# Scores and S^T over 128 contracted rows instead of 96 and 98, in a kernel of attention beside a Fourier transform

## The chip, the core and the metric

The kernel runs on one core of a Trainium2 chip. A core has five engines that run side by side, each with its own queue of instructions: TensorE (PE, matrix products; its loads of the stationary operand are shown apart as PEld), VectorE (DVE), ScalarE (ACT), GpSimd (POOL) and SyncE (SP), whose queue issues this kernel's DMAs. On-chip memory is SBUF, with 128 partitions; products go to PSUM, which has 8 banks of 128 x 512 single-precision numbers. A product multiplies a stationary tile (contracted rows x 128 columns) with a moving tile (contracted rows x up to 512 columns); the contracted rows lie on the partitions.

The metric is the device time of one execution in microseconds, the median of several runs.

## What is computed

Two layers stand side by side in the output: full attention with 32 heads on A, and the real part of a two-dimensional Fourier transform, as products with given matrices, on B. Cut to what matters:

```python
def _A_ref(x, wqkv, wo):                      # x: 1 x 2048 x 1024
    H = 32; Dh = D // H                       # 32 heads of 32
    qkv = (x @ wqkv).reshape(B, S, 3, H, Dh).transpose(2, 0, 3, 1, 4)
    q, k, v = qkv[0], qkv[1], qkv[2]
    p = _softmax(jnp.einsum("bhqd,bhkd->bhqk", q, k) * Dh ** -0.5, axis=-1)
    o = jnp.einsum("bhqk,bhkd->bhqd", p, v)
    return o.transpose(0, 2, 1, 3).reshape(B, S, D) @ wo

def _B_ref(x, dft_seq_re, dft_seq_im, dft_hid_re, dft_hid_im):
    a = jnp.einsum("bsd,ed->bse", x, dft_hid_re)
    b = jnp.einsum("bsd,ed->bse", x, dft_hid_im)
    return jnp.einsum("ts,bse->bte", dft_seq_re, a) - jnp.einsum("ts,bse->bte", dft_seq_im, b)
```

## The kernel before

**The dense products** (q, k, v, the two Fourier stages, the output projection) are Strassen-like products of blocks. Each operand is split into a high and a low part of a shorter float format, and each product of blocks is made of three matmuls (high x high, low x high, high x low) that add up in one PSUM bank: groups of 12 or 24 matmuls, all over 128 rows, issued at line 380. They go by the name of fills, because they are put between the matmuls of the attention.

**The attention** runs head by head. A head's q and k lie in SBUF as three blocks of 32 rows each, so that one product over 96 rows sums the high and low combinations (`qk_d` is laid out for this). There are two sets of tiles, `QS[0]`, `KS[0]` and `QS[1]`, `KS[1]`, of 98 partitions x 2048, and head h uses set h % 2. For each head:

- `scores` (PE line 1185) makes 32 blocks of 128 queries x 1024 keys, two matmuls each, contracted over rows 0 to 95. VectorE takes the negated maximum of each block (line 1191), ScalarE the exponential and its sum (line 1194), in place in the PSUM tile `psS`, of which there are two. For heads after the first, the first four blocks of queries come from a tile of their own, `qx` (96 x 512, loaded at line 1170), because `QS` is still in use by the head two before.
- When the 32 maxima are there, their high and low parts are turned, written to `m_d` and read back into rows 96 and 97 of `QS` (lines 1232 and 1233). Rows 96 and 97 of `KS` hold ones.
- `transposed` (PE line 1308) makes S^T, 64 matmuls of 128 keys x 512 queries, contracted over rows 0 to 97: the last two rows subtract the maximum. ScalarE takes the exponential (line 1312) out of two `psT` banks into SBUF.
- P V (PE line 1327) follows after every four tiles of keys: 32 matmuls in a row, 128 rows x 32 columns stationary, placed in four column groups of the array. Four such sections belong to a head.

While S^T of head h runs, the scores of head h + 1 run too. When the last S^T matmul of head h is done, the loads of q for head h + 2 are issued (four DMAs of 192 KB, line 291), and those of v behind them (line 1285); k was loaded in quarters before.

**The order** of all instructions is written out by a list scheduler in the program, the class `Plan` and the loop from line 1387 on. It knows each operation's cost (a matmul 0.229 us, a score block's maximum 1.22, its exponential 1.235, a DMA's issue 0.46) and what it depends on; at each step it gives TensorE a matmul of the attention if one is ready, and a fill otherwise. The other engines' queues are filled in the same run, in the order of rank and readiness; SP's operations carry the size of the transfer. Each engine's order is then fixed, and the engines wait for each other through semaphores. Memsets and DMAs that are written ahead of the scheduler (lines 279 to 283) or when a pool of tiles is first asked for (`att`, lines 304 to 315) stand in their engine's queue at that place without being in the plan.

Ahead of everything stand the first set of tiles, two memsets on POOL (the ones in `KS[0]` and `rec`, whose right half is only there to fill a transposition), and then the first loads on SP. `att` makes the second set of tiles as soon as the memory of the first stage is free.

Of the kernel before, what the change touches and what calls it, by code (L numbers as in the profile page):

```python
# [8 lines left out]
F32 = mybir.dt.float32  # L9
# [52 lines left out]
class Plan:  # L62
# [23 lines left out]
    def op(self, engine, cost, emit, after=(), uses=(), rank=0.0, kb=0, order=None, other=None, lanes=1, two=False):  # L86

        o = Op(engine, cost, emit, rank, kb, other, two)  # L90
        o.lanes = lanes
        seen = set()
        for d in after:
            if d is not None and id(d) not in seen:
                seen.add(id(d))
                self._wait(o, d)
        for u in uses:
            u.append(o)
        if order is not None:
            p, order.first = order.first, o  # L100
            if p is not None and not p.begun:
                p.soon.append(o)
                o.left += 1
        if o.left == 0:
            self._release(o)
        return o
# [104 lines left out]
def kernel(  # L211
# [19 lines left out]

    r_d = [dram.tile([2 * NS, P], F32, name=f"r_d{h}") for h in range(H)]
    m_d = [dram.tile([2 * NS, P], F32, name=f"m_d{h}") for h in range(H)]

    o_d = [dram.tile([P, 4, NB], F32, name=f"o_d{c}") for c in range(NC)]
    ab_d = [[[dram.tile([P, NB], F32, name=f"ab_d{m}_{e}_{k}") for k in range(NS)] for e in range(2)] for m in range(2)]
# [12 lines left out]
    def f(ap):  # L249
        return ap.bitcast(F32)  # L250
# [25 lines left out]
            nc.sync.dma_start(d[:, 0:2, :] if b % 2 else d[:, 0:3:2, :], f(t).rearrange("p (o n) -> p o n", o=1).broadcast_to([P, 2, NB]))  # L276


    qk0 = tc.alloc_tile_pool(name="qk0", bufs=1, side="right")
    QS, KS = [qk0.tile([98, S], F32R, name="qs0")], [qk0.tile([98, S], F32R, name="ks0")]  # L280
    nc.gpsimd.memset(f(KS[0])[96:98, :], 1.0)
    rec = const.tile([P, 2 * NS], F32, name="rec")
    nc.gpsimd.memset(rec, 1.0)

    def load_qk(h, which, j):
# [18 lines left out]
    def att():  # L304

        if "att" not in late:
            vp.release()
            vph.release()
            late["sums"] = ctx.enter_context(tc.tile_pool(name="sums", bufs=1, reuse_waits="tile"))
            late["atl"] = tc.alloc_tile_pool(name="atl", bufs=1, reuse_waits="tile")  # L310
            late["att"] = a = tc.alloc_tile_pool(name="att", bufs=1, side="right", reuse_waits="tile")
            QS.append(a.tile([98, S], F32R, name="qs1"))
            KS.append(a.tile([98, S], F32R, name="ks1"))
            nc.gpsimd.memset(f(KS[1])[96:98, :], 1.0)
        return late["att"]

# [839 lines left out]
    def load_qk_op(h, which, j, after):  # L1156
        g = h // 4
        got[h, which, j] = op("SP", ISSUE, lambda: load_qk(h, which, j), [*qk_st[2 * g + which][j], *after], [], -2, 192)

    def scores(h):  # L1160
        ST = {}
        sold, suse = small["st"].take()
        maxes, exps = [], []
        if h:
            xold, xuse = qx_r.take()

            def load_x():
                qx["t"] = att().tile([96, NB], F32R, name="qx")
                g, r0 = divmod(h, 4)
                nc.sync.dma_start(f(qx["t"]), qk_d[2 * g][0][r0 * DH : r0 * DH + DH].rearrange("d i c -> (d i) c"))  # L1170

            got[h, "x"] = op("SP", ISSUE, load_x, [*xold, *qk_st[2 * (h // 4)][0], *(att_gate if h == 1 else [])], [xuse], -2, 192)
        qx = {}
        for n, (qt, c) in enumerate([(k % 4, k // 4) for k in range(8)] + [divmod(k, 2) for k in range(8, 32)]):
            old, users = psS_r.take()
            own = h > 0 and qt < 4
            box = {}

            def mm(n=n, qt=qt, c=c, box=box, own=own):
                if n == 0:  # L1180
                    ST["negm"] = sm.tile([P, 2, NS], F32, name="negm", bufs=2)
                    ST["sums"] = sm.tile([P, 2, NS], F32, name="sums", bufs=2)
                box["p"] = p = psS.tile([P, 1024], F32, name="psS")
                for i in range(2):
                    nc.tensor.matmul(  # L1185
                        p[:, i * NB : i * NB + NB], (qx["t"] if own else QS[h % 2][0:96])[:, qt * P : qt * P + P],
                        KS[h % 2][0:96, c * 1024 + i * NB : c * 1024 + i * NB + NB], start=True, stop=True,
                    )

            def mx(qt=qt, c=c, box=box):  # L1190
                nc.vector.tensor_reduce(out=ST["negm"][:, c, qt : qt + 1], in_=box["p"], axis=AX.X, op=ALU.max, negate=True)  # L1191

            def ex(qt=qt, c=c, box=box):
                nc.scalar.activation(box["p"], box["p"], AF.Exp, bias=ST["negm"][:, c, qt : qt + 1], accum_out=ST["sums"][:, c, qt : qt + 1])  # L1194

            a = op("PE", 2 * MM, mm, [*old, got.get((h, "x") if own else (h, 0, qt // 4)), got.get((h, 1, 2 * c)), got.get((h, 1, 2 * c + 1))],
                   [users, xuse] if own else [users])
            b = op("DVE", MAX, mx, [a] + (sold if n == 0 else []), [users, suse], 0)
            e = op("ACT", ES, ex, [b], [users, suse], 0)
            exp_of[a] = e  # L1200
            maxes.append(b)
            exps.append(e)
            Sops.setdefault(h, []).append(a)
            streams["S"].append((a, h, n))
            if n == 5 and h:
                sums(h - 1)

        nold, nuse = small["nm"].take()
        lold, luse = small["lh"].take()
        box = {}  # L1210

        def nmin():
            ST["nm"] = sm.tile([P, NS], F32, name="nm", bufs=2)
            nc.vector.tensor_reduce(out=ST["nm"], in_=ST["negm"].rearrange("p c n -> p n c"), axis=AX.X, op=ALU.min)

        def high():
            box["l"] = sm.tile([P, 2, NS], F32R, name="lh", bufs=2)
            nc.vector.tensor_reduce(out=box["l"][:, 0], in_=ST["negm"].rearrange("p c n -> p n c"), axis=AX.X, op=ALU.min)

        def low():  # L1220
            nc.vector.tensor_tensor(out=box["l"][:, 1], in0=ST["nm"], in1=f(box["l"])[:, 0], op=ALU.subtract)

        b = op("DVE", TINY, high, maxes + lold, [luse, suse], -2)
        a = op("DVE", TINY, nmin, maxes + nold, [nuse, suse], -2)
        c = op("DVE", TINY, low, [a, b], [nuse, luse], -2, two=True)
        def across():
            box["t"] = sm.tile([P, 2 * NS], F32, name="lt", bufs=2)
            nc.vector.transpose(box["t"], f(box["l"]).rearrange("p i s -> p (i s)"))

        d = op("DVE", TINY, across, [b, c], [luse], -2)  # L1230

        put = op("SP", ISSUE, lambda: nc.sync.dma_start(m_d[h].rearrange("i (g p) -> g i p", g=4), box["t"]), [d], [luse], -3, 32)
        moved = [op("SP", ISSUE, lambda: nc.sync.dma_start(f(QS[h % 2])[96:98, :], m_d[h].rearrange("(i q) p -> i (q p)", i=2)), [put], [], -3, 16)]
        mine[h] = (ST, suse, nuse, exps, moved)
# [59 lines left out]
    def transposed(h):  # L1294
# [4 lines left out]
        for t in range(NS):  # L1299
            for j in range(4):  # L1300
                old, users = psT_r.take()
                here = pt_r.n % NPT < NLOW
                pold, puse = pt_r.take()
                box = {}

                def mm(t=t, j=j, box=box):
                    box["p"] = psT.tile([P, NB], F32, name="psT")
                    nc.tensor.matmul(box["p"], KS[h % 2][0:98, t * P : t * P + P], QS[h % 2][0:98, j * NB : j * NB + NB], start=True, stop=True)  # L1308

                def ex(box=box, here=here):  # L1310
                    box["t"] = att_low().tile([P, NB], F32, name="ptl", bufs=NLOW) if here else att().tile([P, NB], F32, name="pt", bufs=NPT - NLOW)
                    nc.scalar.activation(box["t"], box["p"], AF.Exp)  # L1312

                a = op("PE", MM, mm, [*old, *moved, *(att_gate if h == t == j == 0 else []), *(got.get((h, w, k)) for w, k in ((0, j), (1, t // 4)))], [users])
                e = op("ACT", ET, ex, [a, *pold], [users, puse], 0, 0, pt_r)
                exp_of[a] = e
                streams["T"].append((a, h, 4 * t + j))
                Tops.setdefault(h, []).append(a)
                todo.append((t, j, box, e, puse))
# [26 lines left out]
        if h + 2 < H:  # L1346
            for j in range(4):
                load_qk_op(h + 2, 0, j, [Tops[h][-1], Sops[h][-1]])
            load_v(h + 2)
        return e, po, ouse  # L1350

# [145 lines left out]
```

## Time and profile before

| | |
|---|---|
| median of 3 runs | 3041.0 us (3037.66 to 3042.22) |
| the profiled execution | 3036.63 us; its span, first to last instruction, 3034.8 us |
| TensorE busy | 3010.0 us, 14912 matmuls |
| VectorE busy | 2435.1 us |
| ScalarE busy | 2293.7 us |
| POOL busy | 840.5 us |
| mean granted TensorE clock | 0.998 of full speed |
| matmuls of the fills, L380 | 6720, over 128 rows |
| scores, L1185 | 2048, over 96 rows |
| S^T, L1308 | 2048, over 98 rows |
| P V, L1327 | 4096, over 128 rows, 32 columns |

How to read the rows of the profile: a group or a timeline row names the engine, the line of the kernel, the operation, the tile written <- the tiles read, then rows*columns of a matmul's stationary operand and the shape of the moving one, and a count. In the timeline the first number is the start in us from the start of the span, the second the time from the start of the first to the end of the last instruction of that row, and like instructions that follow each other share one row. In a group the numbers behind the bar are the busy time in us, the mean length of one in ns, and the engine's idle time ahead of it with what ended that. Matmuls overlap: one is listed with some 0.39 us from its start to its modelled end, while the next starts well before that. A row of the windows view gives the stretch, its length, each engine's busy time and count, the granted clock, the share of the DMA engines and GB/s. A row of waits gives who waited for whom, the sum in us, how often, and the longest.

### The profile page before, as it was taken

The page shows a single profiled execution, that of the slowest core. Times are in us where ns is not written, and L with a number is a line of the kernel's source. Part 1 is how long each engine was busy: PE and PEld are TensorE (multiplying, and loading weights), DVE is VectorE, ACT ScalarE, POOL GpSimd, SP SyncE. Part 2 cuts the span into 40 slices and gives each one's busy share as a digit, 9 for nine tenths or more (in the row PEclk, how much of TensorE's full clock was granted, in tenths as well). Part 3 has the DMA queues.
Part 4 walks back from the last instruction along what each step waited for, and adds up shares of the span by engine and source line. Part 5 has one row for each costly group of instructions (what it writes and reads, how often), then busy time and mean ns, then how long its engine had stood idle before and what let it go on. Part 6 is the DMA issues. An engine that isn't in the chain of part 4 may idle for free.

```text
span 3034.8 us, 45369 instructions
## 1 busy us (share of the span) xinstructions
PE 3010.0 (99%) x14912; PEld 2149.4 (71%) x14912; DVE 2435.1 (80%) x3283; ACT 2293.7 (76%) x4316; POOL 840.5 (28%) x619
## 2 busy tenths in 40 slices
PE   9999999999999999999999999999999999999999
PEld 7887666667666766677666766676666766676787
DVE  7778789778878877887678888888777889887696
ACT  4347888888888888888888888888888887776331
POOL 2302234322202321231021344332111244332152
PEclk9999999999999999999999999999999999999999
DMA  9974558766615644554434675545433587556662
GB/s 346 352 219 147 181 167 265 243 214 223 222 58 175 204 130 146 187 180 140 139 108 142 207 245 167 163 147 169 126 110 90 158 272 223 157 176 198 228 230 102
DMA packets 376313, 558.06 MB, mean 184 GB/s; under 512 B 110896, under 2 KB 110896, under 8 KB 376016
## 3 DMA queue, kind: packets, MB, share of 16 engines
q1 hardware_dynamic: 376080, 555.17, 57.3%
q8 instruction: 120, 1.97, 0.3%
q14 instruction: 113, 0.93, 0.1%
HBM read 401.93 MB, written 153.09 MB: 183 GB/s over the span
## 4 chain that ended last, share of the span: by engine, by line
PE 92%; DVE 5%; ACT 1%; DMA 1%; issue 1%; POOL 0%; SPq 0%; ACTq 0%; DVEq 0%; POOLq 0%
PE pd L380 41%; PE psT L1308 15%; PE psS L1185 15%; PE pd L1327 14%; PE psT L380 7%; DVE negm L1191 2%; ACT psS L1194 1%; DVE slot L466 1%; DVE raw L444 1%; DVE slot L469 0%; DMA g<-in_ct 0%; DVE h L466 0%; DVE l L469 0%; DMA raw<-in_xb 0%; DVE e L896 0%
## 5 line engine op out<-in xcount | busy, mean ns | idle before, releaser
L1191 DVE TENSOR_REDUCE negm<-psS 128x1 f32<-128x1024 f32 x1024 | 1238.6, 1219 | 207.1 <-PE psS L1185 201.4
L1194 ACT ACTIVATE psS<-psS,negm 128x1024 f32<-128x1024 f32 x1024 | 1140.4, 1114 | 104.5 <-DVE negm L1191 98.5
L1312 ACT ACTIVATE pt<-psT 128x512 f32<-128x512 f32 x1668 | 940.0, 621 | 318.0 <-PE psT L1308 316.7
L380 PE MATMUL pd<-slot,h 128*128 128x512 f32 x3368 | 1168.0, 395 | 1.4 <-DVE h L466 1.4
L1308 PE MATMUL psT<-qs,ks 98*128 98x512 f32 x2048 | 815.3, 403 | 1.3 <-ACT pt L1312 1.3
L380 PEld LDWEIGHTS pd<-slot,h 128*128 128x128 f32 x3368 | 637.4, 189 | 156.8 <-issue 7.5
L380 PE MATMUL pd<-slot,l 128*128 128x512 f32 x1684 | 664.3, 394 | 0.0
L1308 PEld LDWEIGHTS psT<-qs,ks 98*128 98x128 f32 x2048 | 383.9, 189 | 187.5 <-issue 80.5
L1185 PE MATMUL psS<-ks,qs 96*128 96x512 f32 x1552 | 479.7, 398 | 5.9 <-ACT psS L1194 5.5
L1327 PE MATMUL pd<-pt,vt 128*32 128x512 f32 x3336 | 437.2, 596 | 1.3 <-DVE e L670 0.7
L469 POOL TENSOR_TENSOR l<-raw,h 128x512 fp32r<-128x512 f32 x137 | 186.4, 1361 | 825.0 <-PE psT L1308 297.6
L444 POOL TENSOR_TENSOR raw<-raw,g 128x512 f32<-128x512 f32 x215 | 285.0, 1331 | 440.5 <-DMA raw<-in_ct 74.1
L380 PEld LDWEIGHTS pd<-slot,l 128*128 128x128 f32 x1684 | 319.0, 189 | 76.1 <-issue 3.4
L1185 PEld LDWEIGHTS psS<-ks,qs 96*128 96x128 f32 x1552 | 291.7, 189 | 77.7 <-ACT psS L1194 15.5
L469 POOL TENSOR_TENSOR slot<-raw,slot 128x512 fp32r<-128x512 f32 x148 | 212.7, 1444 | 431.7 <-DVE slot L466 291.3
L1327 PEld LDWEIGHTS pd<-pt,vt 128*32 128x32 f32 x3336 | 108.5, 110 | 227.0 <-issue 212.9
L1312 ACT ACTIVATE ptl<-psT 128x512 f32<-128x512 f32 x380 | 219.1, 627 | 59.4 <-PE psT L1308 59.1
L1194 ACT ACTIVATION_READ_ACCUMULATOR psS<-psS,negm 128x1 f32 x1024 | 235.3, 230 | 0.0
L1340 DVE TENSOR_TENSOR ot<-ot,pd 128x512 f32<-128x512 f32 x96 | 65.9, 686 | 169.3 <-PE pd L1327 169.3
L380 PE MATMUL pd<-slot,slot 128*128 128x512 f32 x768 | 194.3, 391 | 0.2 <-DVE ot L1340 0.2
L380 PEld LDWEIGHTS pd<-slot,slot 128*128 128x128 f32 x768 | 144.3, 188 | 31.3 <-DVE ot L1340 0.6
L466 DVE CAST h<-raw 128x512 fp32r<-128x512 f32 x321 | 148.3, 463 | 19.9 <-PE pd L380 16.6
(116 smaller groups left out, 2262.5 us busy)
## 6 DMA issues: line engine op xcount, KB each, us to landing
raw<-in_ct SPq DMA_DIRECT2D x224, 256.0 KB
g<-in_ct SPq DMA_DIRECT2D x128, 256.0 KB
qk_d<-e SPq DMA_DIRECT2D x52, 512.0 KB
qs<-qk_d SPq DMA_DIRECT2D x128, 192.0 KB
ks<-qk_d SPq DMA_DIRECT2D x128, 192.0 KB
raw<-ab_d SPq DMA_DIRECT2D x96, 256.0 KB
c<-u_d SPq DMA_DIRECT2D x88, 256.0 KB
g<-ab_d SPq DMA_DIRECT2D x80, 256.0 KB
```

Source lines behind the costliest of these rows:

```text
L380: nc.tensor.matmul(box["ps"], a[1]((a[0].hi, a[0].lo)[u]()), b[1]((b[0].hi, b[0].lo)[v]()), start=k == 0, stop=k == n - 1)
L444: (nc.gpsimd if e == "POOL" else nc.vector).tensor_tensor(out=dest(), in0=dest() if a is None else a.get(), in1=other["q"] if "q" in other ...
L466: nc.vector.tensor_copy(hi(), raw())
L469: (nc.gpsimd if e == "POOL" else nc.vector).tensor_tensor(out=lo(), in0=raw(), in1=f(hi()), op=ALU.subtract)
L1185: nc.tensor.matmul(p[:, i * NB : i * NB + NB], (qx["t"] if own else QS[h % 2][0:96])[:, qt * P : qt * P + P], KS[h % 2][0:96, c * 1024 + i ...
L1191: nc.vector.tensor_reduce(out=ST["negm"][:, c, qt : qt + 1], in_=box["p"], axis=AX.X, op=ALU.max, negate=True)
L1194: nc.scalar.activation(box["p"], box["p"], AF.Exp, bias=ST["negm"][:, c, qt : qt + 1], accum_out=ST["sums"][:, c, qt : qt + 1])
L1308: nc.tensor.matmul(box["p"], KS[h % 2][0:98, t * P : t * P + P], QS[h % 2][0:98, j * NB : j * NB + NB], start=True, stop=True)
L1312: nc.scalar.activation(box["t"], box["p"], AF.Exp)
L1327: nc.tensor.matmul(po["p"][j * DH : j * DH + DH, :], VT[h][:, k, :], box["t"], start=(k == t0), stop=(k == t), tile_position=(0, j * DH),)
L1340: nc.vector.tensor_tensor(out=po["o"], in0=po["o"], in1=po["p"], op=ALU.add)
```

## The change

`QS` and `KS` get all 128 partitions, and both kinds of product contract over all of them. Rows 96 to 127 are set to zero on POOL when the tiles are made, ahead of the ones in rows 96 and 97 of `KS`. The tile `qx` is no longer taken anew for each head: one tile `QX` of 128 partitions is made with the second set, its rows 96 to 127 set to zero once, and the load of a head writes its rows 0 to 95. As the scores now also multiply rows 96 and 97, and `QS` holds the maxima of the head two before there, an added DMA writes zeros over these rows once that head's S^T is done. The zeros come from a new tensor `z_d` in device memory, filled at the start from `rec`, which is set to zero for this and to one afterwards. The scores that read `QS` depend on this DMA.

```diff
+    z_d = dram.tile([2, S], F32, name="z_d")
...
-    QS, KS = [qk0.tile([98, S], F32R, name="qs0")], [qk0.tile([98, S], F32R, name="ks0")]
+    QS, KS, QX = [qk0.tile([P, S], F32R, name="qs0")], [qk0.tile([P, S], F32R, name="ks0")], []
+    rec = const.tile([P, 2 * NS], F32, name="rec")
+    nc.gpsimd.memset(rec, 0.0)
+    nc.sync.dma_start(z_d.rearrange("i (p c) -> (i p) c", c=2 * NS), rec)
+    nc.gpsimd.memset(f(QS[0])[96:P, :], 0.0)
+    nc.gpsimd.memset(f(KS[0])[96:P, :], 0.0)
     nc.gpsimd.memset(f(KS[0])[96:98, :], 1.0)
-    rec = const.tile([P, 2 * NS], F32, name="rec")
     nc.gpsimd.memset(rec, 1.0)
...
-            QS.append(a.tile([98, S], F32R, name="qs1"))
-            KS.append(a.tile([98, S], F32R, name="ks1"))
+            QS.append(a.tile([P, S], F32R, name="qs1"))
+            KS.append(a.tile([P, S], F32R, name="ks1"))
+            QX.append(a.tile([P, NB], F32R, name="qx"))
+            for t in (QX[0], QS[1], KS[1]):
+                nc.gpsimd.memset(f(t)[96:P, :], 0.0)
             nc.gpsimd.memset(f(KS[1])[96:98, :], 1.0)
...
-                qx["t"] = att().tile([96, NB], F32R, name="qx")
+                att()
                 g, r0 = divmod(h, 4)
-                nc.sync.dma_start(f(qx["t"]), qk_d[2 * g][0][r0 * DH : r0 * DH + DH].rearrange("d i c -> (d i) c"))
+                nc.sync.dma_start(f(QX[0])[0 : 3 * DH], qk_d[2 * g][0][r0 * DH : r0 * DH + DH].rearrange("d i c -> (d i) c"))
...
-                        p[:, i * NB : i * NB + NB], (qx["t"] if own else QS[h % 2][0:96])[:, qt * P : qt * P + P],
-                        KS[h % 2][0:96, c * 1024 + i * NB : c * 1024 + i * NB + NB], start=True, stop=True,
+                        p[:, i * NB : i * NB + NB], (QX[0] if own else QS[h % 2])[:, qt * P : qt * P + P],
+                        KS[h % 2][:, c * 1024 + i * NB : c * 1024 + i * NB + NB], start=True, stop=True,
...
-            a = op("PE", 2 * MM, mm, [*old, got.get((h, "x") if own else (h, 0, qt // 4)), got.get((h, 1, 2 * c)), got.get((h, 1, 2 * c + 1))],
+            a = op("PE", 2 * MM, mm, [*old, *([got.get((h, "x"))] if own else [got.get((h, 0, qt // 4)), got.get((h, "z"))]), got.get((h, 1, 2 * c)), got.get((h, 1, 2 * c + 1))],
...
-                    nc.tensor.matmul(box["p"], KS[h % 2][0:98, t * P : t * P + P], QS[h % 2][0:98, j * NB : j * NB + NB], start=True, stop=True)
+                    nc.tensor.matmul(box["p"], KS[h % 2][:, t * P : t * P + P], QS[h % 2][:, j * NB : j * NB + NB], start=True, stop=True)
...
             for j in range(4):
                 load_qk_op(h + 2, 0, j, [Tops[h][-1], Sops[h][-1]])
+            got[h + 2, "z"] = op("SP", ISSUE, lambda: nc.sync.dma_start(f(QS[h % 2])[96:98, :], z_d), [Tops[h][-1], Sops[h][-1]], [], -2, 16)
             load_v(h + 2)
```

More of the change, by code (lines that the diff above doesn't have):

```diff
@@ L1167, in load_x @@
             def load_x():
-                qx["t"] = att().tile([96, NB], F32R, name="qx")
+                att()
                 g, r0 = divmod(h, 4)
-                nc.sync.dma_start(f(qx["t"]), qk_d[2 * g][0][r0 * DH : r0 * DH + DH].rearrange("d i c -> (d i) c"))
+                nc.sync.dma_start(f(QX[0])[0 : 3 * DH], qk_d[2 * g][0][r0 * DH : r0 * DH + DH].rearrange("d i c -> (d i) c"))
             got[h, "x"] = op("SP", ISSUE, load_x, [*xold, *qk_st[2 * (h // 4)][0], *(att_gate if h == 1 else [])], [xuse], -2, 192)
-        qx = {}
         for n, (qt, c) in enumerate([(k % 4, k // 4) for k in range(8)] + [divmod(k, 2) for k in range(8, 32)]):
```

## The prediction

> **What bounds the kernel now.** I read the page first: the head, the engines' busy times and the chain of work that ended last.
>
> ```profile
> span 3034.8 us, 45369 instructions
> PE 3010.0 (99%) x14912; PEld 2149.4 (71%) x14912; DVE 2435.1 (80%) x3283; ACT 2293.7 (76%) x4316; POOL 840.5 (28%) x619
> PE 92%; DVE 5%; ACT 1%; DMA 1%; issue 1%; POOL 0%; SPq 0%; ACTq 0%; DVEq 0%; POOLq 0%
> ```
>
> TensorE is the bound: it is idle for 3034.8 - 3010.0 = 24.8 us in all, and the chain lies on it for 92%. So little is to be had by taking waits away; the time can only fall if the products follow each other more closely. A matmul's "mean ns" on the page overlaps the next one, so it doesn't say how closely they follow. The starts in the timeline do. First a stretch late in the kernel, in which only products over 128 rows run:
>
> ```profile
> 2899.62 3.33 PE L380 MATMUL psT<-slot,slot 128*128 128x512 f32 x14
> 2902.80 0.39 PE L380 MATMUL pd<-slot,slot 128*128 128x512 f32 x1
> ```
>
> 14 products in 2902.80 - 2899.62 = 3.18 us: one every **227.1 ns**. Now an early stretch of the same kind of products, into which two pairs of score products (96 rows, L1185) are set; no S^T product and no P V product runs yet:
>
> ```profile
> 75.22 1.07 PE L380 MATMUL psT<-slot,slot 128*128 128x512 f32 x4
> 76.13 0.63 PE L1185 MATMUL psS<-ks,qs 96*128 96x512 f32 x2
> 76.60 0.86 PE L380 MATMUL psT<-slot,slot 128*128 128x512 f32 x3
> 77.30 0.63 PE L1185 MATMUL psS<-ks,qs 96*128 96x512 f32 x2
> 77.76 1.31 PE L380 MATMUL psT<-slot,slot 128*128 128x512 f32 x5
> 78.92 1.30 PE L380 MATMUL pd<-slot,slot 128*128 128x512 f32 x5
> ```
>
> Before the first pair 4 products take 0.91 us, 227.5 ns each. From the first pair on, 12 products take 78.92 - 76.13 = 2.79 us, 232.5 ns each, and the 128-row products behind the pairs are as slow as the pairs themselves (0.70 us for 3, 1.16 us for 5). So a product over 96 rows is not slow by itself: it leaves the next few products about 5 ns slower. In the middle of the kernel 96-row, 98-row (S^T, L1308) and 128-row products alternate all the time, and the spacing hardly has time to recover. The windows view gives the counts by stage, and the groups of the stretch from 1500 to 1800 us give the P V products (L1327) to be taken out:
>
> ```profile
> 0.00:250.00 250.00, 243.78 (x1058) 1.00 0.82 283
> 250.00:340.00 90.00, 86.54 (x400) 0.92 0.66 215
> 1500.00:1800.00 300.00, 299.77 (x1526) 1.00 0.55 169
> 2845.00:3035.00 190.00, 185.80 (x819) 1.00 0.57 195
> ```
>
> ```profile
> L1327 PE MATMUL pd<-pt,vt 128*32 128x512 f32 x396 | 51.8, 595 | 0.0
> L1327 PE MATMUL pd<-ptl,vt 128*32 128x512 f32 x84 | 17.6, 595 | 0.2 <-DVE e L896 0.2
> ```
>
> ```profile
> 1504.43 0.39 PE L1308 MATMUL psT<-qs,ks 98*128 98x512 f32 x1
> ...
> 1508.32 0.50 PE L1308 MATMUL psT<-qs,ks 98*128 98x512 f32 x1
> 1508.65 0.64 PE L1185 MATMUL psS<-ks,qs 96*128 96x512 f32 x2
> ```
>
> 396 + 84 = 480 P V products are 15 sections of 32, and one section with the product ahead of it takes 1508.32 - 1504.43 = 3.89 us. That leaves (300 - 15 x 3.89) / (1526 - 480 - 15) = 241.65 / 1031 = **234.4 ns** for each other product, 7.3 ns over the clean spacing, with TensorE idle for 0.2 us of 300 and its clock at 1.00.
>
> **The change part by part.** *The row count.* S and S^T become 128-row products. What of the 7.3 ns goes? Not what the P V sections leave behind. The product after a section starts 1508.65 - 1508.32 = 0.33 us before its follower, 0.10 us late, and this is so for 128-row products too:
>
> ```profile
> 2844.59 0.50 PE L380 MATMUL pd<-slot,h 128*128 128x512 f32 x1
> 2844.93 0.40 PE L380 MATMUL pd<-slot,l 128*128 128x512 f32 x1
> ...
> 2845.86 0.40 PE L380 MATMUL pd<-slot,l 128*128 128x512 f32 x1
> ...
> 2848.62 0.39 PE L380 MATMUL pd<-slot,l 128*128 128x512 f32 x1
> ```
>
> 0.34 us there, between 128-row products alone. The 12 products from 2845.86 on take 2.76 us, 230 ns each, before the clean spacing is back: another 12 x 2.9 = 35 ns. So a section keeps 0.135 us of disturbance whatever the scores do; 15 x 0.135 = 2.0 us of the 7.5 us (1031 x 7.3 ns) in that window. What is left, 5.5 us per 1031 products or 5.3 ns each, I put down to the rows. The products that get it are those outside P V and outside the two clean ends:
>
> ```profile
> L1327 PE MATMUL pd<-pt,vt 128*32 128x512 f32 x3336 | 437.2, 596 | 1.3 <-DVE e L670 0.7 <-DVE e L620 0.6
> L1327 PE MATMUL pd<-ptl,vt 128*32 128x512 f32 x760 | 147.6, 596 | 0.2 <-DVE e L896 0.2
> ```
>
> 14912 - 3336 - 760 - 1058 - 819 = 8,939 products x 5.3 ns = **47 us**. Bounds: 0, if the row count isn't the cause; 8,939 x 7.3 ns less 128 sections x 0.10 us = 52 us, if the products also recover faster behind P V.
>
> *The page's rule against it.* The weight loads have the same length for 128, 98 and 96 rows:
>
> ```profile
> L380 PEld LDWEIGHTS pd<-slot,h 128*128 128x128 f32 x3368 | 637.4, 189 | 156.8 <-issue 7.5
> L1308 PEld LDWEIGHTS psT<-qs,ks 98*128 98x128 f32 x2048 | 383.9, 189 | 187.5 <-issue 80.5
> L1185 PEld LDWEIGHTS psS<-ks,qs 96*128 96x128 f32 x1552 | 291.7, 189 | 77.7 <-ACT psS L1194 15.5
> ```
>
> The Trainium skill, "TensorE: Matmul & The Clock Gate", section "LDWEIGHTS (loading the stationary operand)", says the load goes by columns and the contracted rows don't matter; these rows agree. Its section "Back-to-back issue gap" has no row count in the gap either, and by it this term would be 0; the early stretch above speaks against that, since there only 96-row products were set between. What the row loads say without the page is the first rival below.
>
> *What of the 47 us is given back.* Bounds: nothing and all of it. The order of the products was laid out with 0.229 us for each (line 328). From 234.4 down to 229 the other engines keep the lead the order meant them to have; from 229 to 227.1 TensorE outruns the order, and there, 1.9 of 7.3 or a quarter, new waits on ScalarE and VectorE are to be expected. Now these waits are small:
>
> ```profile
> ACT pt L1312 <- PE psT L1308: 316.7, 235, 5.0
> PEld psS L1185 <- ACT psS L1194: 23.1, 33, 1.7
> ```
>
> ScalarE waits for S^T products 316.7 us in all, TensorE's score loads for ScalarE 23.1 us in 33 cases. I take a fifth of the gain, 9 us, nearer to nothing than to all. Left: **38 us**.
>
> *The start.* The store of zeros to z_d becomes the first DMA of SP's queue and waits for a memset on POOL; all first loads, and so the first product, stand behind it.
>
> ```profile
> 0.73 1.80 POOL L281 MEMSET ks<- 2x2048 f32 x1 [0.29 <-POOLq L1490]
> 0.74 0.39 SPq L428 DMA_DIRECT2D er<-in_wqk  x1
> ```
>
> The first load issues at 0.74. The memset of rec, some 0.1 us, can't start before 0.73, and the store takes one issue of about 0.4 us: the loads come 0.5 to 0.9 us late. TensorE is busy without a break after its start, so this goes through: **+0.7 us** (0 to 2). The two added memsets of 2048 columns (1.80 us each by the row above, which has as many columns) and the second memset of rec, which waits until the store has read it, delay only POOL, and its next work comes late:
>
> ```profile
> 13.98 1.36 POOL L469 TENSOR_TENSOR slot<-er,slot 128x512 fp32r<-128x512 f32 x1 [11.27 <-ACT slot L464]
> ```
>
> It sat idle for 11.27 us; without that cover some 6 us would be lost.
>
> *The second set of tiles.* Three more memsets, 0.45 + 1.80 + 1.80 = 4.1 us, stand on POOL ahead of the one of L314.
>
> ```profile
> 211.26 1.80 POOL L314 MEMSET ks<- 2x2048 f32 x1 [15.18 <-DMA v_d<-stage]
> 218.15 1.28 POOL L469 TENSOR_TENSOR l<-raw,h 128x512 fp32r<-128x512 f32 x1 [5.08 <-DMA qs<-qk_d]
> ```
>
> They would end at 213.06 + 4.1 = 217.2, before POOL's next work at 218.15: 0, at most 4 us if the memory of the new tiles comes free later.
>
> *The clearing of the maxima's rows.* 30 DMAs of 16 KB go into SP's queue behind a head's four loads of qs and ahead of its loads of vt. The scores that read qs now wait for it too. For head 4:
>
> ```profile
> 489.86 2.72 SPq L291 DMA_DIRECT2D qs<-qk_d x4
> ...
> 506.46 0.63 PE L1185 MATMUL psS<-ks,qs 96*128 96x512 f32 x2
> ```
>
> Its first scores from qs come 16 us after these loads; a DMA behind them has about 14 us to land. It costs one issue on SP, of which the chain holds 0%: 0. If it were late, ScalarE and VectorE would starve behind the scores.
>
> *The order.* It is computed anew with 30 more operations, so every small wait is dealt anew: 24.8 us of idle time, give or take a fifth, +-5 us, 0 in the mean.
>
> **Sum.** The profiled execution took 3036.6 us with a span of 3034.8; the median of the three runs is 3041.0, 4.4 us (0.15%) above it. 3036.6 - 47 + 9 + 0.7 = 2999, and 4.4 us on that is 3004 beside the median.
>
> **Rivals.** *The row count is not the cause.* S and S^T differ from the others in more than rows: each is a group by itself, first and last product in one, into other banks, with its own waits and signals. If one of these disturbs the spacing, 128 rows change nothing: 3041 + 0.7, with +-5 us from the order. For it speaks that 96 and 98 rows disturb alike and that P V, with 128 rows, does too (0.135 us above); against it that the clean stretches change banks and wait as well (the row of 2902.80 goes to another bank at the same spacing), and hold the 227 ns.
>
> *The gain is given back.* TensorE outruns ScalarE and VectorE, which are busy for 76% and 80% of the span, and the loop from scores over the maximum and the exponential back to the scores' bank becomes the bound in many places. If more than half of the 47 us goes so: about 3041 - 20 = 3021. Against it: the 316.7 us that ScalarE waits for S^T.
>
> *Slower: the clock.* TensorE paused at the head of the attention, and then its clock was halved (windows again; TensorE's busy time comes first, the clock third from the end):
>
> ```profile
> 250.00:254.00 4.00, 2.67 (x11) 1.54 (x9) 3.72 (x4) 3.04 (x7) 3.22 (x3) 1.00 0.85 284
> 254.20:264.40 10.20, 9.62 (x23) 0.50 0.65 209
> ```
>
> 1.3 us of idle time, then 10.2 us at clock 0.50, which cost 5.1 us: 6.4 us for one such episode. A new order with pauses over a microsecond has more of them. With the row gain it would take six to be slower; without it one is enough, and two give 3041 + 13 = 3054. Against it: the window of 1500 to 1800 us shows none.
>
> **How the numbers follow.** The forecast, 2987 to 3015, has 0.55; the gain given back, up to 3035, 0.18; no row effect, 3035 to 3047, 0.17; slower by the clock 0.10. No change is what lies within 0.2%, 6 us, of 3041, about what a measurement of this kernel can tell. Faster: 0.55 + 0.18 + 0.01 of the third case = 0.74; same 0.15; slower 0.10 + 0.01 = 0.11. The range goes from 2987, all of the upper bound with nothing given back (3041 - 52 - 2), to 3046, no row effect with the worst order.
>
> **What would show it.** Right: between P V sections some ten products after a section, rows of the timeline a steady 227 ns apart through scores and S^T, and a window of 300 us that holds some 20 more products; TensorE's idle time up from 24.8 to some 35 us. Wrong: (300 us - sections) / products still at 234 ns, with all rows 128; that is the first rival. Spacing at 227 but idle time on TensorE up by over 25 us is the second; rows of clock 0.50 past 400 us the third. A first product later than 8.2 us would falsify the start, scores waiting on the clearing DMA the covering of 14 us.

## The result, and the profile after

The changed kernel takes 2996.93 us in the median (2991.34 to 3000.05, 4 runs) against 3039.33 us for the kernel before beside it (3035.83 to 3042.22): a ratio of 0.9859, 95% interval 0.9838 to 0.9879, or 42 us less. Its profiled execution took 2999.43 us, with a span of 2997.6. The head of the page and its chain of waits:

```profile
span 2997.6 us, 45469 instructions
PE 2966.3 (99%) x14912; PEld 2130.0 (71%) x14912; DVE 2428.4 (81%) x3265; ACT 2294.0 (77%) x4316; POOL 874.8 (29%) x643
PE 89%; DVE 5%; DMA 2%; ACT 2%; issue 1%; SPq 0%; POOL 0%; ACTq 0%; DVEq 0%; POOLq 0%
```

The same 14912 matmuls keep TensorE busy for 43.7 us less (3010.0 - 2966.3), while its idle time rose from 24.8 to 31.3 us. VectorE and ScalarE are busy as long as before, within 7 us. So the time came out of the distance between matmuls. The early stretch with two pairs of scores among fills, in the timeline:

```profile
74.93 0.62 PE L1193 MATMUL psS<-ks,qs 128*128 128x512 f32 x2
75.39 0.84 PE L389 MATMUL psT<-slot,slot 128*128 128x512 f32 x3
76.07 0.62 PE L1193 MATMUL psS<-ks,qs 128*128 128x512 f32 x2
76.52 1.29 PE L389 MATMUL psT<-slot,slot 128*128 128x512 f32 x5
77.65 2.66 PE L389 MATMUL pd<-slot,slot 128*128 128x512 f32 x11
```

The same 12 products take 77.65 - 74.93 = 2.72 us, 226.7 ns each, where they took 2.79 us. From row to row it is 0.46, 0.68, 0.45 and 1.13 us for 2, 3, 2 and 5 products: the fills behind the scores are no slower than any others.

Two things still make the spacing uneven. The P V sections disturb, as forecast, here with 128 rows throughout:

```profile
1518.13 3.64 PE L1335 MATMUL pd<-pt,vt 128*32 128x512 f32 x32
1521.70 0.73 PE L1316 MATMUL psT<-qs,ks 128*128 128x512 f32 x2
1522.27 1.08 PE L1193 MATMUL psS<-ks,qx 128*128 128x512 f32 x4
1523.19 0.39 PE L389 MATMUL pd<-slot,l 128*128 128x512 f32 x1
```

Two products take 0.57 us behind the section, 0.12 us more than two clean ones, and the next four 230 ns each. The second had no term in the forecast, which counts the waits of TensorE but not what a wait leaves behind it. One such wait, with the row of the load (PEld) that waited for ScalarE:

```profile
1506.14 0.39 PE L1316 MATMUL psT<-qs,ks 128*128 128x512 f32 x1
...
1509.99 0.39 PE L389 MATMUL pd<-slot,h 128*128 128x512 f32 x1
1510.40 0.30 PEld L1193 LDWEIGHTS psS<-ks,qx 128*128 128x128 f32 x2 [0.45 <-ACT psS L1202]
1510.41 0.73 PE L1193 MATMUL psS<-ks,qx 128*128 128x512 f32 x2
1510.98 0.39 PE L389 MATMUL pd<-slot,h 128*128 128x512 f32 x1
...
1513.98 0.61 PE L389 MATMUL pd<-slot,h 128*128 128x512 f32 x2
```

From 1506.14 to 1509.99 lie 17 products, 226.5 ns each. The scores of 1510.41 come 0.42 us after the fill ahead of them, 0.19 us late; the pair takes 0.57 us, 0.12 us more than a clean one, and the 13 products from 1510.98 to 1513.98 take 230.8 ns each. So this pause of 0.19 us costs about another 0.12 + 13 x 0.004 = 0.17 us behind it.

The waits that grew are those of the scores for ScalarE, in the groups of the page:

```profile
L1193 PE MATMUL psS<-ks,qs 128*128 128x512 f32 x1552 | 472.0, 393 | 12.3 <-ACT psS L1202 11.8
```

and in the waits view (who, for whom, sum in us, how often, longest):

```profile
PEld psS L1193 <- ACT psS L1202: 35.7, 50, 2.5
```

TensorE's idle time ahead of these scores was 5.9 us before the change (the groups of its page), and the loads of their stationary operand waited 23.1 us in 33 cases; now it is 12.3, and 35.7 us in 50 (in a second profile of the changed kernel 8.1, and 30.1 us in 47). TensorE is ahead of ScalarE more often.

### The profile page after: what moved, and what is told of

Its sections match the earlier page's. It is cut to its first block, busy times and chain, and to the rows that moved or that the text cites. A ratio compares the mean times of both kernels' runs of the same rounds, so it can differ in the third digit from the quotient of the medians.

```text
span 2997.6 us, 45469 instructions
## 1 busy us (share of the span) xinstructions
PE 2966.3 (99%) x14912; PEld 2130.0 (71%) x14912; DVE 2428.4 (81%) x3265; ACT 2294.0 (77%) x4316; POOL 874.8 (29%) x643
## 4 chain that ended last, share of the span: by engine, by line
PE 89%; DVE 5%; DMA 2%; ACT 2%; issue 1%; SPq 0%; POOL 0%; ACTq 0%; DVEq 0%; POOLq 0%
PE pd L389 40%; PE psT L1316 15%; PE psS L1193 14%; PE pd L1335 14%; PE psT L389 7%; DVE negm L1199 2%; ACT psS L1202 1%; DVE raw L453 1%; DVE slot L475 1%; DMA qs<-qk_d 0%; DMA g<-ab_d 0%; DVE h L475 0%; DVE slot L478 0%; DMA qk_d<-e 0%; DMA raw<-ab_d 0%
## 5 line engine op out<-in xcount | busy, mean ns | idle before, releaser
L389 PE MATMUL pd<-slot,h 128*128 128x512 f32 x3368 | 1149.5, 390 | 0.8 <-DVE ot L1348 0.6
L1316 PE MATMUL psT<-qs,ks 128*128 128x512 f32 x2048 | 804.6, 398 | 1.3 <-ACT pt L1320 1.3
L389 PE MATMUL pd<-slot,l 128*128 128x512 f32 x1684 | 656.5, 390 | 0.0
L1316 PEld LDWEIGHTS psT<-qs,ks 128*128 128x128 f32 x2048 | 380.7, 188 | 191.7 <-issue 83.8
L1193 PE MATMUL psS<-ks,qs 128*128 128x512 f32 x1552 | 472.0, 393 | 12.3 <-ACT psS L1202 11.8
L478 POOL TENSOR_TENSOR l<-raw,h 128x512 fp32r<-128x512 f32 x145 | 196.8, 1357 | 790.5 <-DVE h L475 370.4
L1193 PEld LDWEIGHTS psS<-ks,qs 128*128 128x128 f32 x1552 | 287.8, 188 | 84.4 <-ACT psS L1202 26.0
L1202 ACT ACTIVATION_READ_ACCUMULATOR psS<-psS,negm 128x1 f32 x1024 | 245.7, 240 | 0.0
L389 PEld LDWEIGHTS pd<-slot,slot 128*128 128x128 f32 x768 | 144.2, 188 | 31.3 <-DVE ot L1346 0.6
L475 DVE CAST h<-raw 128x512 fp32r<-128x512 f32 x321 | 152.8, 477 | 15.3 <-PE pd L389 12.3
```

The source lines that it names most:

```text
L389: nc.tensor.matmul(box["ps"], a[1]((a[0].hi, a[0].lo)[u]()), b[1]((b[0].hi, b[0].lo)[v]()), start=k == 0, stop=k == n - 1)
L475: nc.vector.tensor_copy(hi(), raw())
L478: (nc.gpsimd if e == "POOL" else nc.vector).tensor_tensor(out=lo(), in0=raw(), in1=f(hi()), op=ALU.subtract)
L1193: nc.tensor.matmul(p[:, i * NB : i * NB + NB], (QX[0] if own else QS[h % 2])[:, qt * P : qt * P + P], KS[h % 2][:, c * 1024 + i * NB : c * ...
L1316: nc.tensor.matmul(box["p"], KS[h % 2][:, t * P : t * P + P], QS[h % 2][:, j * NB : j * NB + NB], start=True, stop=True)
```

## The experiments

My theory: what disturbs is a product whose number of contracted rows differs from its neighbours'. Rivals: another part of the change or the new order brings the gain; only one of the two kinds of product matters; a count below 128 is slow in itself; the disturbance goes with how many rows are missing. Five kernels are built from the changed one with another range of rows alone. The scheduler knows nothing of row counts, so the order of their instructions is that of the changed kernel.

### Everything but the rows

```diff
-                        p[:, i * NB : i * NB + NB], (QX[0] if own else QS[h % 2])[:, qt * P : qt * P + P],
-                        KS[h % 2][:, c * 1024 + i * NB : c * 1024 + i * NB + NB], start=True, stop=True,
+                        p[:, i * NB : i * NB + NB], (QX[0] if own else QS[h % 2])[0:96, qt * P : qt * P + P],
+                        KS[h % 2][0:96, c * 1024 + i * NB : c * 1024 + i * NB + NB], start=True, stop=True,
...
-                    nc.tensor.matmul(box["p"], KS[h % 2][:, t * P : t * P + P], QS[h % 2][:, j * NB : j * NB + NB], start=True, stop=True)
+                    nc.tensor.matmul(box["p"], KS[h % 2][0:98, t * P : t * P + P], QS[h % 2][0:98, j * NB : j * NB + NB], start=True, stop=True)
```

> All that the change adds stays (128-partition tiles, memsets, the store of zeros, the 30 clearing DMAs, the new order), but scores contract rows 0 to 95 and S^T rows 0 to 97 again. Row theory: the whole gain is gone, ratio to before 0.998 to 1.004 (3034 to 3050 us), the early stretch with score pairs back at 232 to 233 ns per product, and some 1527 products in a window of 300 us without waits. Rival (the gain came from the new order or from the other parts of the change): the time stays near that of the changed kernel, 2997 us, ratio 0.986.

Measured: 3040.73 us, ratio to before 1.0014 (1.0004 to 1.0024). The page's head, the first and the last row of the early stretch (12 products lie between the starts), and one window of 300 us of this kernel:

```profile
span 3034.1 us, 45441 instructions
PE 3011.9 (99%) x14912; PEld 2151.1 (71%) x14912; DVE 2429.8 (80%) x3265; ACT 2299.5 (76%) x4316; POOL 876.3 (29%) x643
```

```profile
75.61 0.63 PE L1193 MATMUL psS<-ks,qs 96*128 96x512 f32 x2
...
78.39 1.98 PE L389 MATMUL pd<-slot,slot 128*128 128x512 f32 x8
```

```profile
900.00:1200.00 300.00, 299.59 (x1518) 1.00 0.53 164
```

The same window of the changed kernel:

```profile
900.00:1200.00 300.00, 299.35 (x1548) 1.00 0.53 164
```

The whole gain is gone: 12 products take 2.78 us again, and the window holds 30 matmuls fewer (12 of them are P V: 468 against 480 by the groups of the two). The medians differ by 3040.73 - 2996.93 = 44 us (by the two ratios to before, 1.0014 and 0.9859, 47 us). Not all of this is the distance between products: the mean granted clock was 0.996 to 0.998 in the runs of this kernel and 0.998 or 0.999 in those of the changed one, on average 0.002 lower, which for a busy TensorE is an estimated 6 us of 3040. The kernel with 127 rows below is free of this. All the rest, with the new order, costs 0.1% here, some 4 us by the ratio. This pair has the same order, so its pages show what was given back: TensorE's busy time falls by 3011.9 - 2966.3 = 45.6 us, its idle time rises from 22.2 to 31.3, by 9 us.

### One kind of product at a time

First S^T goes back to 98 rows, and the scores stay at 128 (in the diffs from here on only the operands that change are shown):

```diff
-                    nc.tensor.matmul(box["p"], KS[h % 2][:, t * P : t * P + P], QS[h % 2][:, j * NB : j * NB + NB], start=True, stop=True)
+                    nc.tensor.matmul(box["p"], KS[h % 2][0:98, t * P : t * P + P], QS[h % 2][0:98, j * NB : j * NB + NB], start=True, stop=True)
```

> Scores over 128 rows, S^T over 98. Row theory: the early stretch (scores and fills alone) is clean at 227 ns; each S^T product still disturbs the few behind it, some 27 ns in all where fills follow, and with 2048 of them spread among the fills that takes most of the gain: 3025 to 3037 us. Rival (only the 96-row products, a quarter of the array's rows unused, matter): 2997 us. Rival (only the 98-row products matter): 3040 us.

Then the scores go back to 96, and S^T stays at 128:

```diff
-(QX[0] if own else QS[h % 2])[:, qt * P : qt * P + P]
-KS[h % 2][:, c * 1024 + i * NB : c * 1024 + i * NB + NB]
+(QX[0] if own else QS[h % 2])[0:96, qt * P : qt * P + P]
+KS[h % 2][0:96, c * 1024 + i * NB : c * 1024 + i * NB + NB]
```

> S^T over 128 rows, scores over 96. Row theory: early stretch at 232 to 233 ns as before; 1024 pairs of scores at some 32 ns of disturbance each are 33 us of the gain at most: 3012 to 3030 us, and the last stretch of the attention, where S^T and fills run alone, clean at 227 ns. Rival (only the 98-row products matter): 2997 us. Rival (only the 96-row products matter): 3040 us.

Measured: with scores alone at 128 rows 3034.41 us, ratio 0.9985 (0.9976 to 0.9994); with S^T alone at 128 rows 3023.91 us, ratio 0.9953 (0.9938 to 0.9968). Each kind disturbs, and both lie in the ranges of the row theory; neither gives 2997 or 3040. The two gains, 0.15% and 0.47%, do not add up to 1.41% (against the kernel with the old rows and the same order they are 0.29% and 0.61% of 1.55%). This would follow if disturbances that overlap among the fills cost once, so that most comes back only with the last of them; no run here isolates that. What each kind does alone shows in the timeline in two places. The early stretch, first with scores at 128 rows, then with scores at 96 (12 products each):

```profile
76.17 0.61 PE L1193 MATMUL psS<-ks,qs 128*128 128x512 f32 x2
...
78.89 1.29 PE L389 MATMUL pd<-slot,slot 128*128 128x512 f32 x5
```

```profile
75.66 0.63 PE L1193 MATMUL psS<-ks,qs 96*128 96x512 f32 x2
...
78.44 1.75 PE L389 MATMUL pd<-slot,slot 128*128 128x512 f32 x7
```

2.72 us against 2.78. And the last head, where the scores are over and S^T alternates with fills alone, the same 21 products in both, first with S^T over 98 rows, then over 128:

```profile
2778.84 0.39 PE L1316 MATMUL psT<-qs,ks 98*128 98x512 f32 x1
...
2783.73 0.40 PE L1316 MATMUL psT<-qs,ks 98*128 98x512 f32 x1
```

```profile
2775.03 0.39 PE L1316 MATMUL psT<-qs,ks 128*128 128x512 f32 x1
...
2779.79 0.39 PE L1316 MATMUL psT<-qs,ks 128*128 128x512 f32 x1
```

4.89 us, 232.9 ns each, against 4.76 us, 226.7 ns. In this stretch only the rows of S^T differ.

### One row short of 128

The four operands of scores and S^T:

```diff
-(QX[0] if own else QS[h % 2])[:, qt * P : qt * P + P]
-KS[h % 2][:, c * 1024 + i * NB : c * 1024 + i * NB + NB]
+(QX[0] if own else QS[h % 2])[0:127, qt * P : qt * P + P]
+KS[h % 2][0:127, c * 1024 + i * NB : c * 1024 + i * NB + NB]
...
-KS[h % 2][:, t * P : t * P + P], QS[h % 2][:, j * NB : j * NB + NB]
+KS[h % 2][0:127, t * P : t * P + P], QS[h % 2][0:127, j * NB : j * NB + NB]
```

> Scores and S^T over 127 rows; the result is the same, as row 127 is zero. If any count other than 128 disturbs the products behind it: 3034 to 3048 us, early stretch at 232 to 233 ns. If the disturbance goes with the number of rows left out: 1 of 30 leaves nothing to see, 2995 to 3000 us and 227 ns.

Measured: 3036.76 us, ratio 0.9995 (0.9986 to 1.0005). The early stretch of this kernel:

```profile
76.02 0.63 PE L1193 MATMUL psS<-ks,qs 127*128 127x512 f32 x2
...
78.81 1.52 PE L389 MATMUL pd<-slot,slot 128*128 128x512 f32 x6
```

2.79 us, 232.5 ns each. One missing row disturbs as much as 32. This kernel's mean granted clock, 0.998 to 1.000, was no lower than that of the changed one, so the two compare without the clock: 3036.76 - 2996.93 = 40 us in the medians (41 us by the two ratios), and 3009.9 - 2966.3 = 43.6 us of TensorE's busy time, by the head of this kernel's page:

```profile
span 3036.2 us, 45469 instructions
PE 3009.9 (99%) x14912; PEld 2143.7 (71%) x14912; DVE 2435.0 (80%) x3265; ACT 2298.5 (76%) x4316; POOL 878.4 (29%) x643
```

Why the clock of the kernel with 96 and 98 rows was lower isn't shown; a count that differs from the neighbours' doesn't bring it by itself, since the kernel with 127 rows has one too. In both profiles TensorE pauses for 1.33 us at the head of the attention (ahead of its scores at 252.82 and 253.24 us); behind that pause stand some 10 us at half the clock with 96 and 98 rows (first row), and none with 127 (second row):

```profile
250.00:270.00 20.00, 18.47 (x58) 0.74 0.63 208
250.00:270.00 20.00, 17.12 (x73) 1.00 0.69 232
```

### All at 98 rows

The operands of scores and S^T get 0:98 in the places where the last kernel has 0:127, and those of the fills:

```diff
-a[1]((a[0].hi, a[0].lo)[u]()), b[1]((b[0].hi, b[0].lo)[v]())
+a[1]((a[0].hi, a[0].lo)[u]())[0:98], b[1]((b[0].hi, b[0].lo)[v]())[0:98]
```

> Every product outside P V contracts rows 0 to 97, the fills too, which leaves 30 of 128 rows of each dense product out; all neighbours have the same count again, but none has 128. If it is the change of the count from one product to the next that disturbs: 227 ns in the clean ends and between P V sections, 2990 to 3005 us. If any count below 128 is slow: the stretch of fills alone at 232 ns or more, and 10,816 products at 5 to 10 ns more each than in the changed kernel, 3050 to 3100 us.

This kernel leaves 30 of the 128 rows out of each dense product. Measured: 3003.64 us, ratio 0.9892 (0.9877 to 0.9907). The early stretch and a stretch of fills alone, all over 98 rows:

```profile
76.45 0.62 PE L1193 MATMUL psS<-ks,qs 98*128 98x512 f32 x2
...
79.17 1.07 PE L389 MATMUL pd<-slot,slot 98*128 98x512 f32 x4
...
2879.75 1.52 PE L389 MATMUL psT<-slot,slot 98*128 98x512 f32 x6
2881.11 3.11 PE L389 MATMUL pd<-slot,slot 98*128 98x512 f32 x13
```

2.72 us for the 12 products, and 1.36 us for 6, both 226.7 ns each. So 98 rows are as quick as 128 as long as all neighbours have 98: it is the change of the count that costs, not a count below 128. These fills still have the P V sections, over 128 rows, between them. The median is 6.7 us above that of the changed kernel, and the mean granted clock, 0.995 to 0.997, is 0.0025 lower on average: by an estimate 7.5 us of 3000, enough for the difference.

### Laying the order out for the new spacing

```diff
-    MM, PV, SWITCH, TINY = 0.229, 0.866, 0.19, 0.17
+    MM, PV, SWITCH, TINY = 0.227, 0.866, 0.19, 0.17
```

> The changed kernel with the measured spacing, 0.227 us instead of 0.229, as a matmul's cost in the order's plan. If part of the gain is given back because TensorE outruns an order laid out for 0.229 us: TensorE's idle time of 31 us falls by some 5 to 10 us, 2988 to 2992 us. Rival (the waits are chance of the order): 2992 to 3002 us, idle time 25 to 40 us.

```diff
-    MM, PV, SWITCH, TINY = 0.229, 0.866, 0.19, 0.17
+    MM, PV, SWITCH, TINY = 0.227, 0.866, 0.19, 0.17
...
-    LATE = 0.25
+    LATE = 0.35
```

> As mm227, and a matmul of the attention is placed only 0.35 us after the plan has its operands ready, instead of 0.25. If waits on ScalarE at the score tiles are what is given back, they get fewer: idle time of TensorE ahead of L1193 below 8 us (12 in the changed kernel), 2985 to 2992 us. Rival (chance of the order): 2992 to 3002 us.

The first measured 2992.97 us, ratio 0.9852 (0.9839 to 0.9866), in the rival's range. The second measured 3022.41 us, ratio 0.9951 (0.9939 to 0.9964), outside all that was expected. Its windows and waits between 2820 and 2890 us show most of the loss:

```profile
2820.00:2890.00 70.00, 52.90 (x214) 0.85 0.65 229
```

```profile
POOL slot L478 <- ACT slot L473: 106.9, 7, 97.3
PE psT L389 <- ACT slot L473: 11.3, 2, 10.4
```

TensorE is idle for 17.1 of 70 us where the output projection begins, its clock falls to 0.85, and POOL and TensorE wait for ScalarE's casts of the projection's operands. TensorE's idle time ahead of the scores of line 1193 that read qs did fall below 8 us, to 7.8, but the order came out badly elsewhere.

The changed kernel and the first of the two were run once more, on one chip:

> The changed kernel once more, on one chip with the next: ratio to before 0.984 to 0.988, beside which mm227 is judged.

> The order laid out with 0.227 us, once more. If the earlier 4 us were real: again 3 to 6 us below the changed kernel of this call, intervals of the two ratios apart. If chance: within 2 us of it.

Measured: 2997.21 us, ratio 0.9871 (0.9854 to 0.9887), and 2992.02 us, ratio 0.9857 (0.9842 to 0.9873). The order laid out with 0.227 us has the lower median both times, by 4 and 5 us, but the intervals overlap. TensorE's idle time by the pages was 26.3 and 32.8 us with 0.227, 31.3 and 27.6 us without, so the predicted fall by 5 to 10 us is not to be seen. The mean granted clock was 0.999 or 1.000 in the runs with 0.227 and 0.998 or 0.999 in those without, on average 0.001 higher, an estimated 3 us of the 4 to 5. It is the fastest kernel by its medians; that the new spacing in the plan makes it so is not shown.

## Why the prediction came out

The forecast was 3004 us; 2996.93 was measured. Step by step:

- **The cause.** The forecast put the slow spacing down to the row count, against the rival that other traits of scores and S^T disturb. The kernel with all the added parts and the old rows has none of the gain, and the one with 127 rows has none either, though groups, banks, waits and signals are as in the changed kernel. The Trainium skill, "TensorE: Matmul & The Clock Gate", section "Back-to-back issue gap", gives the gap by columns alone. The kernel with 98 rows throughout agrees (226.7 ns, as with 128); where the count changes, the measurement decides against it.
- **Its size.** 47 us were forecast. With the same order, TensorE's busy time differs by 45.6 us from the kernel with 96 and 98 rows, part of it clock, and by 43.6 us from the one with 127 rows, where the clock is the same; the medians differ by 44 and 40 us. So the term was a few us too large. The sign that I gave, some 20 more products in a window of 300 us, depends on the window. From 900 to 1200 us the changed kernel holds 1548, 22 more than the kernel before (1526). A later window holds 4 fewer than before:

```profile
1500.00:1800.00 300.00, 297.63 (x1522) 1.00 0.56 177
```

By the groups of that stretch 464 of them are P V products, 16 fewer than before, and the others are 12 more, in spite of 2.4 us of idle time. So the other products are the ones to count. Outside P V, the window from 900 us gives (300 - 15 x 3.89) / (1548 - 480 - 15) = 229.5 ns, with its 390 + 90 products of P V by the groups of that stretch: between 227.1 and 234.4, as what P V leaves would have it (2.0 ns per product) with some of the waits.
- **What a P V section leaves.** Part of the 0.135 us was read off 12 products that stand behind something else as well. Between the rows that the forecast shows, a load of TensorE waits for VectorE:

```profile
2845.52 0.19 PEld L380 LDWEIGHTS pd<-slot,h 128*128 128x128 f32 x1 [0.40 <-DVE ot L1340]
```

The size holds all the same: behind the section of 1518.13 in the changed kernel it is 0.12 us for the first two products and 0.01 us for the next four. That it came out of those rows is luck.
- **What is given back.** 9 us were taken, a fifth, from the part of the gain by which TensorE outruns the order. With the same order, the idle time rose by 9.1 us from the kernel with 96 and 98 rows (22.2) and by 5.0 us from the one with 127 (3036.2 - 3009.9 = 26.3), to 31.3. In a second profile of the changed kernel it was 27.6 us, so 1 to 9 us is what the profiles bear out. That it comes from TensorE outrunning the order's 0.229 us was only argued: the runs with 0.227 us show no clear fall of the idle time.
- **The start**, forecast at +0.7 us, was wrong in its premise. The store to z_d did not become SP's first DMA:

```profile
0.74 0.12 POOL L284 MEMSET rec<- 128x32 f32 x1 [0.29 <-POOLq L1499]
0.75 0.39 SPq L437 DMA_DIRECT2D er<-in_wqk  x1
1.20 0.41 SPq L285 DMA_DIRECT2D z_d<-rec  x1
...
6.25 0.79 PE L389 MATMUL psT<-slot,h 128*128 128x512 f32 x1 [6.25 <-ACT slot L473]
```

The first load goes ahead of it, at 0.75 us, and the first product starts at 6.25 instead of 6.22 us. I read the order off the source. Lines that stand ahead of the hand-written order need not stand first in their engine's queue, as I had it in the section on the kernel; what put the load first isn't shown.
- **The second set of tiles** costs nothing, as forecast, though not at the times I gave: the first memset starts earlier, and the last ends before POOL's next work can begin.

```profile
202.38 0.53 POOL L322 MEMSET qx<- 32x512 f32 x1 [7.56 <-PE pd L389]
...
213.29 1.81 POOL L323 MEMSET ks<- 2x2048 f32 x1
216.38 1.28 POOL L478 TENSOR_TENSOR l<-raw,h 128x512 fp32r<-128x512 f32 x1 [1.28 <-DVE h L475]
```

- **The clearing DMA** stays covered. For head 4 it is issued at 486.65, and the first scores that read qs start 11.6 us later. In the whole profile no product waits for this DMA.

```profile
483.28 3.32 SPq L297 DMA_DIRECT2D qs<-qk_d  x4
486.65 0.28 SPq L1357 DMA_DIRECT2D qs<-z_d  x1
...
498.29 0.61 PE L1193 MATMUL psS<-ks,qs 128*128 128x512 f32 x2
```

- **The order** was given 0 +- 5 us. Order and added parts together cost some 4 us in the kernel with the old rows, by its ratio of 1.0014 to before, and nothing in the one with 127 rows (0.9995).
- **The clock** rival didn't decide, but it isn't nothing. Away from the two ends of the span, TensorE ran at half its clock for two stretches of 3.4 us in the changed kernel's profile (from 251.7 and from 2422.6 us on; the second is the sign past 400 us that I gave), and for 10.2 + 3.4 us in that of the kernel before. Half of the difference, an estimated 3 us of the 37 by which the span fell, came from this and not from the spacing; the sum has no term for it.
- **The total.** The sum put the profiled execution at 2999 us, and it took 2999.43. So close is luck: the rows gave some 3 us less than forecast, not more and perhaps less was given back, and the clock added 3 us that no term held. The forecast for the median was off by 7 us, mostly because it put the median 4.4 us above the profiled execution, as before the change; it came out 2.5 us below.

## What to carry to other kernels

Look at the starts of successive matmuls, not only at their lengths. The mean lengths on the page fell by 5 ns for fills and attention alike (395 to 390, 403 to 398, 398 to 393); only the starts show which neighbours cause it, and that the products behind them pay too. Where TensorE is the bound and products of different row counts alternate, give them all the same count, with zero rows; half the job brought little here (0.15% and 0.47% for the halves, 1.41% for both). The price here, zero rows and a small DMA per head to clear rows that are used for something else, was between nothing and 0.1% (the ratios 0.9995 and 1.0014 of the kernels that pay it without the gain).

## What the runs showed of the hardware

- A change of the number of contracted rows between successive matmuls leaves the next few some 5 ns slower each, two pairs of scores among fills 0.06 to 0.07 us in all (2.78 and 2.79 against 2.72 us); 127 beside 128 does as much as 96, and 98 throughout runs at the 226.7 ns of 128 throughout. The mechanism within TensorE is not seen in any of these runs.
- Products are also spaced more widely behind a P V section (128 rows, 32 columns; 0.57 us for two, then 230 ns each) and behind a wait of TensorE (230.8 ns each for 13, behind 1510.41). Whether that is the same mechanism isn't shown.
- With one order and the same pause of 1.33 us, one profile has some 10 us at half the clock behind it and another none (0.74 and 1.00 from 250 to 270 us). A few us between two kernels can be the clock, and the mean granted clock of each run tells.
